# A third of a fused kernel's loads moved to ScalarE's DMA queue, with a new written order of all stages

## The chip, the cores and the metric

The kernel runs on one core of a Trainium2 chip. A core has TensorE (PE in the profile; its weight loads are PEld), VectorE (DVE), ScalarE (ACT), GpSimd (POOL) and SyncE (SP), each with its own instruction queue, and 16 DMA engines that all queues share. Times are device microseconds (us) of one execution, lower is better.

## The reference

Two operations follow each other. The first is a linear attention with a decaying state, for 4 sequences of 768 steps, 8 heads of 48 channels:

```python
for t in range(S):
    cur = einsum('bhd,bhe->bhde', u[None] * kt, vt)
    y[:, :, t] = einsum('bhd,bhde->bhe', rt, state + cur)
    state = w[None, :, :, None] * state + einsum('bhd,bhe->bhde', kt, vt)
```

Its output, with the 8 heads side by side as `x` of 4 x 768 x 384, goes through a gated layer. `conv` is a causal convolution with 5 taps over the steps, each channel by itself:

```python
gate = sigmoid(conv(x, conv_w))
out  = (gate * (x @ w_val)) @ w_out
```

Inputs and output are float32. `r`, `k` and `v` are 4.7 MB each, `w_val` and `w_out` 0.6 MB each, the output 4.7 MB.

## The kernel before, in words

**Tiling.** The 768 steps of each sequence are cut into 3 units of 256 steps, 12 units in all (`n` = 0 to 11), and each unit into two chunks of 128 steps. The state passes from chunk to chunk within a sequence; a new sequence starts at n = 0, 3, 6 and 9.

**One unit.** The loads bring `r` (one transfer of 384 KB), and `k` and `v` (two transfers of 192 KB each, one for each chunk: `k:4.1` is the second half of unit 4). In memory a row of 48 channels is 192 bytes, so a `k` or `v` transfer is 1,024 pieces of 192 bytes; `r` takes two steps in one piece, 1,024 pieces of 384 bytes. Then: `RS` and `KS` multiply `r` and `k` with powers of the decay (L260, L289, on POOL; with a star in the order on DVE). `RT` and `KT` transpose them on PE (L274, L312), `RE` and `KE` copy the result out of PSUM on ACT (L282, L322). `PR`, `S` and `SE` make the factor of the bonus term `u` (L331, L343, L355), `DV` multiplies `v` with it (L358, POOL, with a star DVE). `CV` casts `v` (L298, ACT). `A` makes the scores of a chunk (L372, PE), `M` masks them (L385, DVE, four for each unit). `KV` forms the chunk's part of the state (L399, PE), `ZE` and `ID` decay and add (L416, L411, DVE). `YD` starts the output of both chunks from `DV` (L427, PE), `Y` completes a chunk (L441, PE), `YE` copies it out (L470, ACT). Of the gated layer `C` is the convolution (L485, 40 small matmuls), `SG` the sigmoid (L498, ACT), `V` the value product (L505 and L514), `HT` gate times value (L527, DVE), `O` the output product (L537), `OE` its copy (L549, ACT), and `st` the store of a unit (L553, SP). The last unit does the gated layer in smaller parts (`CL`, `GL`, `VL`, `HL`, `OL`, `XL`, `stl`).

**Beginning.** `w` and `cw` load the decay row and the convolution weights on SP; `wt` and `ut` load small pairs on ACT; `WB`, `LN`, `DRI` and `DKI` make the tables of decay powers (PE, then ACT). Unit 0 runs in halves (`RSP`, `RTP`, `REP`, `KSP`, `KTP`, `KEP`). `Wv` and `Wo` load the two weight matrices, `WV`, `WP` and `WO` cast them. `CWB`, `CWT`, `CWC`, `CWD` prepare the convolution weights (`CWB`, on DVE, is the first to need `cw`). `TL` loads the sigmoid's table on ACT.

**What sets the order.** `ORDER` is a written list of all 555 stages. A loop at the end calls them one by one, and each appends its instructions to the queues of its engines. So the list fixes the order within every queue, and nothing across queues: an instruction starts when its queue has come to it and the semaphores that it waits for have arrived. A load on SP is passed by no other load of SP, but may run long before or after the compute stages that stand beside it in the list. The function `queue` sends a load to ScalarE's queue when its token has a star, else to SyncE's. Such an issue stands in the same queue as ACT's copies and sigmoids.

**Buffers.** There are 7 buffers each for `k` and `v`, 6 for `r`, 11 for output units, and 8 PSUM banks handed out in turn. By the trace's issue records the transfers use 8 completion semaphores in turn, over both queues: an issue also waits until the transfer before it on the same semaphore has landed. For example, the issue of `k:1.1` starts at 4.19 us, and the first half of `r:0`, which had the same semaphore, landed at 4.17 us.

Of the kernel before, what the change touches and what calls it, by code (L numbers as in the profile page):

```python
# [16 lines left out]
def kernel(  # L17
# [14 lines left out]
    B, H, S, D = r.shape  # L32
    C = 128
# [60 lines left out]
    wt = consts.tile([128, NP], F32)  # L94
    nc.vector.memset(wt, 1.0)
    ut = consts.tile([128, NP], F32)
# [28 lines left out]
    st = {}  # L125
# [522 lines left out]
    def store_l(n, cl, half, eng):  # L648
# [3 lines left out]
        eng.dma_start(out=out[b, t0 : t0 + C, c0 : c0 + n0], in_=st["o_l", n, cl, half])  # L652

    ORDER = """
        w wt:0 r:0.0 WB:0 wt:1 r:0.1 cw r:1* CWB WB:1 LN:0 k:0.0 DRI:0 k:0.1 LN:1 ut:1 k:1.1 DKI:0
        k:1.0 DRI:1 RSP:0.0 ut:0 RSP:0.1 CWT RS:1 RTP:0.1 DKI:1 WCT r:2 REP:0.1 k:2.1 k:2.0
        RTP:0.0 v:0.0 v:0.1 v:1.1 v:1.0 r:3 REP:0.0 KSP:0.0 KSP:0.1 WCM Wv k:3.1 v:2.0 UW k:3.0
        v:2.1 Wo k:4.0 RS:2 k:4.1 r:4 KTP:0.0 v:3.0 v:3.1 r:5 KEP:0.0 RT:1 KS:1* KTP:0.1 KEP:0.1
        A:0.0 k:5.1 KS:2 PR:0 M:0.0 k:5.0 r:6 RE:1 KT:1 S:0 A:0.1 PR:1 v:4.0 v:4.1 SE:0 M:0.1 KE:1
        S:1 A:1.1 k:6.0 k:6.1 v:5.0 v:5.1 A:1.0 M:0.3 SE:1 DV:0 r:7 DV:1 RT:2 M:1.3 M:1.2 CWC KT:2  # L660
        M:0.2 CV:0 KV:0.0 RS:3 M:1.1 RE:2 ZE:0.0 WV CV:1 YD:0 M:1.0 KE:2 TL KV:0.1 ZE:0.1 KV:1.0
        ID:1.0 KS:3 YD:1 A:2.0 PR:2 Y:0.1 ZE:1.0 Y:1.0 Y:0.0 YE:0.1 Y:1.1 k:7.1 CWD YE:1.0 A:2.1
        RT:3 KV:1.1 YE:0.0 YE:1.1 C:1 M:2.1 ZE:1.1 V:0.1 RE:3 S:2 SG:1.0 M:2.3 CV:2 M:2.2 C:0
        V:1.0 SE:2 SG:0.0 SG:1.1 SG:0.1 M:2.0 DV:2 HT:1.0 KV:2.0 V:0.0 ID:2.0 WO KT:3 YD:2 V:1.1
        k:7.0 ZE:2.0 v:7.1 HT:1.1 v:6.0 PR:3 KE:3 HT:0.1 WP Y:2.0 Y:2.1 O:1.0 KS:4 O:1.1 HT:0.0
        S:3 YE:2.0 A:3.1 RS:4 OE:1.0 YE:2.1 OE:1.1 SE:3 A:3.0 M:3.1 CV:3 v:6.1 C:2 SG:2.0 RT:4
        O:0.1 SG:2.1 DV:3 M:3.2 RS:5 v:7.0 KV:3.0 KS:5 RS:6 M:3.0 KT:4 V:2.1 RE:4 O:0.0 M:3.3 KE:4
        YD:3 ZE:3.0 KV:3.1 Y:3.1 Y:3.0 OE:0.1 PR:4 HT:2.1 ZE:3.1 A:4.1 A:4.0 RT:5 YE:3.1 OE:0.0
        M:4.3 S:4 V:2.0 SE:4 YE:3.0 M:4.0 M:4.1 r:8 DV:4 RE:5 k:8.1 KT:5 CV:4 C:3 RT:6 PR:5 M:4.2
        KV:4.0 V:3.1 SG:3.0 ID:4.0 YD:4 ZE:4.0 SG:3.1 k:8.0 S:5 KS:6 Y:4.0 SE:5 Y:4.1 KE:5 A:5.0  # L670
        YE:4.0 HT:3.1 YE:4.1 A:5.1 HT:2.0 v:8.0 M:5.1 M:5.2 RE:6 C:4 KT:6 CV:5 O:2.1 DV:5 V:4.0
        M:5.3 KV:4.1 M:5.0 SG:4.0 SG:4.1 YD:5 PR:6 k:9.0 OE:2.1 KE:6 k:9.1 KV:5.0 RS:7 ZE:4.1
        V:3.0 RT:7 S:6 ID:5.0 SE:6 ZE:5.0 KS:7 RE:7 O:2.0 Y:5.0 Y:5.1 HT:3.0 A:6.0 A:6.1 OE:2.0
        DV:6 HT:4.0 KT:7 M:6.0 V:4.1 YE:5.0 M:6.3 RS:8 O:3.0 HT:4.1 O:3.1 YE:5.1 KE:7 CV:6 C:5
        PR:7 A:7.1 OE:3.0 M:6.2 A:7.0 M:6.1 V:5.0 SG:5.0 OE:3.1 M:7.3 S:7 M:7.0 SG:5.1 SE:7 KS:8
        KV:6.0 V:5.1 ZE:6.0 HT:5.1 YD:6 O:4.1 KV:6.1 r:9 HT:5.0 RT:8 M:7.2 v:8.1 Y:6.1 k:10.1 CV:7
        Y:6.0 DV:7 r:10* ZE:6.1 RE:8 KS:9 KV:7.0 O:5.1 YE:6.0 KT:8 M:7.1 v:9.1 O:4.0 OE:5.1 O:5.0
        YD:7 OE:4.1 ID:7.0 PR:8 YE:6.1 RS:9 OE:4.0 KE:8 S:8 k:10.0 ZE:7.0 r:11 KV:7.1 OE:5.0 SE:8
        Y:7.1 Y:7.0 v:9.0 v:11.1 YE:7.1 CV:8 A:8.0 A:8.1 C:6 DV:8 M:8.0 v:10.0 V:6.1 M:8.2 SG:6.1
        v:10.1 ZE:7.1 KT:9 YE:7.0 k:11.1 M:8.3 HT:6.1 V:6.0 RT:9 SG:6.0 k:11.0 YD:8 HT:6.0 M:8.1  # L680
        KV:8.0 ID:8.0 O:6.0 RE:9 KE:9 C:7 ZE:8.0 RS:10 PR:9 Y:8.0 RS:11 Y:8.1 OE:6.0 A:9.0 A:9.1
        SG:7.1 KS:10 SG:7.0 RT:10 YE:8.1 M:9.1 v:11.0 M:9.3 YE:8.0 S:9 SE:9 M:9.2 DV:9 CV:9 M:9.0
        V:7.1 C:8 RE:10 KV:9.0 O:6.1 HT:7.1 V:7.0 KT:10 RT:11 HT:7.0 V:8.0 ZE:9.0 st:5 OE:6.1
        V:8.1 KV:9.1 SG:8.1 SG:8.0 CV:10 PR:10 O:7.1 RE:11 O:7.0 ZE:9.1 KV:10.0 HT:8.1 YD:9 S:10
        Y:9.0 KS:11 KE:10 OE:7.1 Y:9.1 YE:9.0 ID:10.0 SE:10 DV:10 HT:8.0 st:2 ZE:10.0 YE:9.1
        A:10.1 M:10.3 A:10.0 CV:11 C:9 M:10.1 KV:10.1 M:10.2 OE:7.0 KT:11 SG:9.1 V:9.0 PR:11 O:8.1
        KE:11 SG:9.0 OE:8.1 O:8.0 M:10.0 ZE:10.1 KV:11.0 V:9.1 YD:10 OE:8.0 S:11 Y:10.1 HT:9.0
        YE:10.1 SE:11 ID:11.0 st:1 ZE:11.0 Y:10.0 HT:9.1 st:4 st:3 A:11.1 DV:11 A:11.0 M:11.1
        YE:10.0 C:10 M:11.2 M:11.0 O:9.0 V:10.1 st:7 YD:11 SG:10.1 st:8 SG:10.0 HT:10.1 V:10.0
        Y:11.0 HT:10.0 O:9.1 st:0 M:11.3 YE:11.0 O:10.1 OE:10.1 Y:11.1 OE:9.1 VL:11.0 YE:11.1  # L690
        OE:9.0 CL:11.0 GL:11.0 CL:11.1 HL:11.0 O:10.0 GL:11.1 VL:11.1 HL:11.1 st:6 OE:10.0 OL:11.0
        st:9 OLb:11.1 OLa:11.1 XL:11.0 st:10 stl:11.0 XLb:11.1 XLa:11.1 stl:11.1 stl:11.2
    """

    wct = consts.tile([128, NP], F32)
# [136 lines left out]
```

## Time and profile before

| | |
|---|---|
| median of 5 runs | 104.85 us (104.12 to 105.15) |
| the profiled execution | 104.12 us |
| its span, first to last instruction | 102.3 us, so 1.8 us lie around it |
| ACT, DVE and POOL busy | 73.1, 72.6 and 65.8 us |
| loads and stores | 15.35 MB read from HBM, 4.72 MB written |
| big loads (r, k, v, the two weights) | 63: 61 issued by SP, 2 by ACT (`r:1`, `r:10`) |
| last load issued, landed | 76.19 us, 80.78 us (`v:11.0`) |
| last matmul ends | 98.4 us |

All times within the execution are counted from the start of the span. "Busy" of PE is modelled from pipelined matmuls. Of the 40 slices of the page each is 2.56 us long. The DMA share is the time that packets took, over 16 engines; it passes 1 where packets overlap.

### The profile page before, as it was taken

Reading aid. Unit: us, or ns where it says so; the run is one execution under the profiler, and the core shown is the slowest. Engines: PE = TensorE matmul, PEld = TensorE weight load, DVE = VectorE, ACT = ScalarE, POOL = GpSimd, SP = SyncE. Lnnn points to the kernel's source line nnn. Section 1 sums busy time; section 2 is a strip of 40 time slices with the busy share of each in tenths; the row PEclk is TensorE's granted clock in tenths of the full one; section 3 lists DMA queues with packets and bytes.
Section 4 is the critical chain, followed back from the end, with each engine's and each line's share of the span. In section 5 each row is a group of like instructions: output and inputs, shape, how many; then the busy total and the mean of one; then the engine's idle time right before and its main releaser. Section 6 shows DMA issues by size and latency. Waiting matters only on the chain.

```text
span 102.3 us, 4626 instructions
## 1 busy us (share of the span) xinstructions
PE 85.1 (83%) x2017; PEld 70.2 (69%) x2017; DVE 72.6 (71%) x145; ACT 73.1 (71%) x126; POOL 65.8 (64%) x67
## 2 busy tenths in 40 slices
PE   1425969369969889999989999996999999999940
PEld 1224759249869678799858796785889788986720
DVE  4058799767537794899959998497697697984320
ACT  5476744595886699798968949968898986636730
POOL 7969298299878687979756269599597660500000
PEclk9999999975999999999999999999999999999996
DMA  0999999998979989999979899899899994372471
GB/s 5 265 211 177 228 186 189 289 222 152 298 135 253 207 174 225 200 165 211 171 139 241 167 211 242 173 193 205 172 180 227 382 345 175 116 270 87 154 276 34
DMA packets 67504, 20.36 MB, mean 199 GB/s; under 512 B 63510, under 2 KB 67484, under 8 KB 67484
## 3 DMA queue, kind: packets, MB, share of 16 engines
q1 hardware_dynamic: 64428, 19.18, 88.2%
q10 hardware_dynamic: 3056, 0.89, 4.0%
q8 instruction: 15, 0.25, 1.1%
q14 instruction: 5, 0.04, 0.1%
HBM read 15.35 MB, written 4.72 MB: 196 GB/s over the span
## 4 chain that ended last, share of the span: by engine, by line
PE 49%; SPq 15%; DMA 14%; ACT 8%; issue 4%; POOL 3%; DVE 2%; POOLq 0%
SPq L69 13%; DMA v_st<-in_v_dram 11%; PE bank L441 9%; PE bank L485 9%; PE bank L537 6%; PE bank L505 5%; PE bank L274 3%; PE bank L427 3%; DMA r_st<-in_r_dram 3%; POOL dv L358 3%; ACT xT L470 2%; PE bank L514 2%; PE bank L372 2%; PE bank L312 2%; PE bank L399 2%
## 5 line engine op out<-in xcount | busy, mean ns | idle before, releaser
L385 DVE TENSOR_TENSOR at<-bank,mask 128x512 bf16<-128x512 f32 x48 | 30.9, 681 | 3.4 <-PE bank L372 3.3
L260 POOL TENSOR_TENSOR rs<-r_st,dr 128x768 bf16<-128x768 f32 x11 | 20.2, 1834 | 6.2 <-DMA r_st<-in_r_dram 6.2
L358 POOL TENSOR_TENSOR dv<-v_st,s_sb 128x768 bf16<-128x768 f32 x12 | 17.7, 1478 | 9.6 <-DVE s_sb L355 5.2
L289 POOL TENSOR_TENSOR ks<-k_st,dk 128x768 bf16<-128x768 f32 x10 | 18.2, 1822 | 6.6 <-DMA k_st<-in_k_dram 4.5
L282 ACT COPY rT<-bank 128x1024 bf16<-128x1024 bf16 (+1 forms) x13 | 15.9, 1234 | 3.8 <-PE bank L274 3.8
L322 ACT COPY kT<-bank 128x1024 bf16<-128x1024 bf16 (+1 forms) x13 | 12.5, 959 | 5.4 <-PE bank L537 1.8
L527 DVE TENSOR_TENSOR hT<-bank,gate 128x384 bf16<-128x384 f32 x22 | 11.8, 551 | 3.6 <-PE bank L514 2.3
L470 ACT CAST xT<-bank 128x384 bf16<-128x384 f32 x24 | 11.1, 487 | 4.1 <-PE bank L441 4.1
L537 PE MATMUL bank<-wout,hT 128*128 128x384 bf16 x66 | 13.4, 327 | 0.0
L298 ACT CAST vb<-v_st 128x768 bf16<-128x768 f32 x12 | 10.0, 836 | 4.2 <-DMA v_st<-in_v_dram 4.2
L498 ACT ACTIVATE gate<-bank 128x384 bf16<-128x384 f32 x22 | 10.0, 494 | 2.5 <-PE bank L485 2.3
L485 PE MATMUL bank<-xT,cwd 64*64 64x128 bf16 (+1 forms) x440 | 11.3, 244 | 0.5 <-ACT xT L470 0.4
L505 PE MATMUL bank<-xT,wval 128*128 128x256 bf16 x66 | 10.8, 273 | 1.0 <-issue 0.9
L549 ACT COPY o_sb<-bank 128x384 f32<-128x384 f32 x22 | 10.7, 500 | 1.2 <-PE bank L537 1.2
L485 PEld LDWEIGHTS <-cwd 64*64 64x64 bf16 x440 | 9.8, 106 | 1.9 <-issue 1.0
L372 PE MATMUL bank<-rT,kT 48*128 48x128 bf16 x192 | 9.2, 236 | 1.0 <-ACT kT L322 0.7
L312 PE MATMUL bank<-ident,ks 128*128 128x128 bf16 x96 | 8.8, 242 | 1.3 <-DVE ks L289 1.3
L441 PE MATMUL bank<-at,vb 128*32 128x128 bf16 x384 | 9.9, 235 | 0.0
L331 DVE TENSOR_TENSOR pr<-bank,rT 128x1024 bf16<-128x1024 bf16 (+1 forms) x13 | 8.3, 644 | 1.9 <-ACT kT L322 1.3
L274 PE MATMUL bank<-ident,rs 128*128 128x128 bf16 x96 | 8.6, 242 | 1.2 <-DVE rs L260 1.1
L312 PEld LDWEIGHTS <-ks 128*128 128x128 bf16 x96 | 6.7, 109 | 2.4 <-POOL rs L260 1.3
L399 PE MATMUL bank<-vb,ks 128*128 128x96 bf16 x80 | 6.8, 209 | 1.8 <-ACT vb L298 1.8
(80 smaller groups left out, 138.2 us busy)
## 6 DMA issues: line engine op xcount, KB each, us to landing
k_st<-in_k_dram SPq DMA_DIRECT2D x24, 192.0 KB, 5.2
v_st<-in_v_dram SPq DMA_DIRECT2D x24, 192.0 KB, 4.5
out_dram<-o_sb SPq DMA_DIRECT2D x11, 384.0 KB, 4.6
r_st<-in_r_dram SPq DMA_DIRECT2D x9, 384.0 KB, 5.7
r_st<-in_r_dram ACTq DMA_DIRECT2D x2, 384.0 KB, 5.4
wv_st<-in_moe_w_val_dram SPq DMA_DIRECT2D x1, 576.0 KB, 6.8
wo_st<-in_moe_w_out_dram SPq DMA_DIRECT2D x1, 576.0 KB, 5.1
r_st<-in_r_dram SPq DMA_DIRECT2D x2, 192.0 KB, 3.2
```

The costliest lines, as they stand in the source:

```text
L69: eng.dma_start(out=d[n][:, cl], in_=src[b, :, t0 : t0 + C, :].transpose([1, 0, 2]))
L260: eng.tensor_tensor(out=rs_t[n % 2][:, :, ps[0] : ps[1], :, 0:D].rearrange("p s n a d -> p (n a) s d"), in0=r_st[n][:, hs], in1=dr[:, hs], ...
L282: nc.scalar.copy(out=st["rT", n][:, ps[0] : ps[1], :].rearrange("x n (i s) -> x s n i", s=2), in_=st["r_tr", n, ps[0]],)
L289: eng.tensor_tensor(out=ks_t[n % 3][:, cs, :, :, 0:D].rearrange("p c n a d -> p c (n a) d"), in0=k_st[n][:, cs], in1=dk[:, cs], op=ALU.mult,)
L312: nc.tensor.transpose(tr[:, c, p, :], ks[:, cls[0] + c, p].rearrange("p a x -> p (a x)"), ident,)
L358: eng.tensor_tensor(out=dv_t[n % 2].rearrange("p c (h d) -> p (c h) d", d=D), in0=v_st[n].rearrange("p c h d -> p (c h) d"), in1=st["s", n ...
L385: nc.vector.tensor_tensor(out=st["at", n, cl][:, par], in0=st["at_ps", n, cl][par], in1=mask[:, None, :].to_broadcast([128, NP, 128]), op= ...
L441: nc.tensor.matmul(out=y_ps[32 * q : 32 * q + 32, T, :], lhsT=lt, rhs=rh, start=False, stop=last, skip_group_check=True,)
L470: nc.scalar.copy(out=xT_t[b % 2][:, :, t0 : t0 + C], in_=st["y_ps", n, cl])
L485: nc.tensor.matmul(out=g_ps[i][64 * qo : 64 * qo + 64, o0 : o0 + n0], lhsT=cwd[rows, T, t, :], rhs=xT[rows, T, t0 + c0 + t : t0 + c0 + t + ...
L505: nc.tensor.matmul(out=v_ps[:, 0:W], lhsT=wval[:, kt, i, :], rhs=xT[:, kt, t0 : t0 + W], start=(kt == 0), stop=(kt == NT - 1), skip_group_ ...
L537: nc.tensor.matmul(out=o_ps, lhsT=hT[:, i, c0 : c0 + C], rhs=wout[:, k, :], start=(j == 0), stop=(j == 2),)
```

## The change

Nothing but `ORDER` changes: the same 555 tokens, in another order, and 19 more of them with a star. No function and no tile changes.

**Queues.** ScalarE issues 19 of the 63 big loads in place of 2: `r:1 k:2.1 k:2.0 r:4 k:3.1 v:2.1 k:4.1 v:3.1 k:5.1 r:5 k:6.1 v:6.1 k:7.1 v:7.1 r:10 k:10.1 v:9.0 v:10.1 v:10.0`, in this order. SyncE keeps 44. Besides, `RS:4` and `DV:6` go from POOL to DVE (`KS:1` was there before).

**Order.** Every stage moves. The tokens of SP's loads, which stood far ahead of the compute stages in the list, stand later in it. `cw` and `CWB` come later, `wt:0` too; `r:1` is ACT's first load, ahead of `wt` and `ut`; three stores (`st:3`, `st:4`, `st:1`) stand beside the last loads of `v`. The diff, cut:

```diff
-        w wt:0 r:0.0 WB:0 wt:1 r:0.1 cw r:1* CWB WB:1 LN:0 k:0.0 DRI:0 k:0.1 LN:1 ut:1 k:1.1 DKI:0
-        k:1.0 DRI:1 RSP:0.0 ut:0 RSP:0.1 CWT RS:1 RTP:0.1 DKI:1 WCT r:2 REP:0.1 k:2.1 k:2.0
-        RTP:0.0 v:0.0 v:0.1 v:1.1 v:1.0 r:3 REP:0.0 KSP:0.0 KSP:0.1 WCM Wv k:3.1 v:2.0 UW k:3.0
...
-        YD:7 OE:4.1 ID:7.0 PR:8 YE:6.1 RS:9 OE:4.0 KE:8 S:8 k:10.0 ZE:7.0 r:11 KV:7.1 OE:5.0 SE:8
-        Y:7.1 Y:7.0 v:9.0 v:11.1 YE:7.1 CV:8 A:8.0 A:8.1 C:6 DV:8 M:8.0 v:10.0 V:6.1 M:8.2 SG:6.1
...
+        w r:1* ut:1 r:0.0 ut:0 r:0.1 WB:0 WB:1 wt:1 LN:0 DRI:0 RSP:0.0 LN:1 DRI:1 DKI:0 DKI:1
+        k:0.1 RSP:0.1 RTP:0.1 k:0.0 k:1.1 KSP:0.1 k:1.0 wt:0 r:2 REP:0.1 k:2.1* KTP:0.1 RS:1 cw
+        RTP:0.0 KEP:0.1 REP:0.0 KSP:0.0 k:2.0* RT:1 KTP:0.0 KS:1* A:0.1 v:0.0 KT:1 WCT UW KEP:0.0
+        RE:1 A:0.0 PR:0 S:0 M:0.2 M:0.3 v:0.1 KE:1 v:1.1 CWB WCM A:1.1 PR:1 RS:2 SE:0 M:0.0 M:1.2
+        TL M:1.3 M:0.1 A:1.0 v:1.0 S:1 r:3 KS:2 CWT DV:0 SE:1 CV:0 r:4* KT:2 Wv k:3.0 KV:0.0 M:1.1
...
+        PR:7 Y:6.1 YE:6.0 YE:6.1 A:7.1 A:7.0 KS:9 O:5.1 S:7 M:7.2 r:10* OE:5.1 k:10.0 SE:7 M:7.0
+        C:6 DV:7 M:7.3 M:7.1 RT:9 CV:7 SG:6.1 S:8 k:10.1* SE:8 RE:9 KV:7.0 V:6.1 ID:7.0 ZE:7.0
+        KT:9 YD:7 HT:6.1 k:11.0 SG:6.0 V:6.0 PR:9 KV:7.1 KE:9 Y:7.1 Y:7.0 HT:6.0 r:11 YE:7.1
+        ZE:7.1 RS:10 A:8.0 A:8.1 A:9.0 YE:7.0 C:7 M:8.3 O:5.0 CV:8 v:9.1 v:9.0* k:11.1 M:8.0 M:9.1
+        KS:10 SG:7.0 O:6.0 DV:8 SG:7.1 M:9.0 RT:10 OE:5.0 OE:6.0 KV:8.0 M:8.2 M:8.1 S:9 V:7.0
+        V:7.1 RE:10 ID:8.0 SE:9 ZE:8.0 v:10.1* O:6.1 OE:6.1 KT:10 RS:11 KE:10 v:10.0* YD:8 A:9.1
...
+        DV:10 M:10.3 ZE:9.0 M:10.0 SG:8.1 v:11.1 st:4 V:8.1 v:11.0 KV:9.1 ZE:9.1 O:7.0 PR:11
```

## The prediction

> **What bounds the kernel now.** First I read the page: the busy shares, the granted clock and the DMA row over the 40 slices.
>
> ```profile
> span 102.3 us, 4626 instructions
> ...
> PE 85.1 (83%) x2017; PEld 70.2 (69%) x2017; DVE 72.6 (71%) x145; ACT 73.1 (71%) x126; POOL 65.8 (64%) x67
> ...
> PEclk9999999975999999999999999999999999999996
> DMA  0999999998979989999979899899899994372471
> ```
>
> No engine but PE is above 71%, and the DMA row is near full until about 80 us. So two things run close together: the loads, and PE. The windows cut the execution where PE becomes dense (21.67), where its clock is full for good (25.40) and where its last matmul ends.
>
> ```profile
> 0.00:21.67 21.67, 11.73 (x122) 9.46 (x122) 13.56 (x33) 13.11 (x21) 15.45 (x36) 1.00 1.16 199
> 21.67:25.40 3.73, 3.73 (x114) 3.27 (x114) 3.33 (x5) 2.80 (x5) 3.73 (x3) 0.54 0.92 153
> 25.40:98.50 73.10, 69.67 (x1790) 57.48 (x1782) 55.67 (x108) 56.88 (x101) 46.62 (x30) 1.00 0.90 205
> ```
>
> The first number pair in each row after the length is PE's busy time. From 25.40 on PE idles only 73.10 - 69.67 = 3.4 us. Before 21.67 it idles 9.9 us and does 122 of its 2,017 matmuls. In the second row the clock is 0.54 of full: some 1.7 us of PE's time are lost there. Hence the end of the kernel is the moment at which PE becomes dense, plus a fixed amount of PE work (about 72 us at full clock for what is left at 21.67), plus PE's later idling, plus a tail of 4 us (last matmul 98.4, span 102.3).
>
> What sets that moment is in the chain of work in order of time, and in SP's timeline beside it.
>
> ```profile
> 14.15 5.82 DMA v_st<-in_v_dram
> ...
> 20.14 1.49 POOL dv L358
> ...
> 21.67 0.55 PE bank L427 x6
> ```
>
> ```profile
> 2.58 4.51 SPq L69 DMA_DIRECT2D k_st<-in_k_dram  x4
> 7.13 1.02 SPq L76 DMA_DIRECT2D r_st<-in_r_dram  x1
> 8.20 2.22 SPq L69 DMA_DIRECT2D k_st<-in_k_dram  x2
> 10.46 4.69 SPq L69 DMA_DIRECT2D v_st<-in_v_dram  x4
> ```
>
> The last of the four `v` halves of units 0 and 1 is issued at 14.15, lands at 19.98, POOL multiplies it until 21.62, and `YD:1` opens PE's dense stretch. The loads stand one behind another on SP at 1.0 to 1.2 us each; the first two took 0.42 and 0.58, so later issues are held back by transfers before them.
>
> **The change, part by part.** The sum is made against the profiled execution (104.12, span 102.3, 1.82 around it) and carried to the median of the runs shown, which is 0.73 higher.
>
> *The beginning.* In SP's queue the two `k:2` issues (2.22 us) leave the place ahead of `v`, and `cw` (0.40) comes in: `v:1.0` is issued up to 1.8 us earlier. If SP's issuing were the limit, PE would be dense 1.8 us sooner. If the 16 engines are, nothing is won: `r:0, r:1, k:0, k:1, r:2, k:2, v:0, v:1` have to pass in both orders. The DMA share is 1.35 at 10 to 13 us and 1.42 at 13 to 16, so the engines are the nearer row. A loss is possible too: `r:4` is now issued by ACT after `CV:0` (16.7 us in before) and takes half of the engines while `v:1.0` finishes, at worst 1.8 us. Range -1.8 to +1.8. I take -0.6, for the queue that is not blocked and for this wait, which goes away because `CWB` leaves the head of DVE's queue:
>
> ```profile
> DVE cw5b L223 <- DMA cw<-in_moe_conv_w_dram: 2.9, 1, 2.9
> ```
>
> It let `RSP:0.0` start only at 5.79, though its table (`DRI:0`) was ready at 4.99 and `r` at 4.17; next late is `DRI:1` and the first `k` half, so 0.8 us at most move on.
>
> *19 loads on ACT.* The row for one in mid-run is `r:10`:
>
> ```profile
> 58.44 0.47 ACT L549 COPY o_sb<-bank 128x384 f32<-128x384 f32 x1
> 58.49 0.40 ACTq L76 DMA_DIRECT2D r_st<-in_r_dram  x1
> 58.80 0.51 ACT L498 ACTIVATE gate<-bank 128x384 bf16<-128x384 f32 x1
> ```
>
> The issue takes 0.40 and lies beside the copy; the sigmoid starts 0.36 after the copy, as copies do without an issue between. So 17 more issues of 0.40 to 0.47 are 7 to 8 us of ACT's sequencer, hidden behind the running copy. I take 0. Without that cover, with about half of them on PE's path, it is +3.4 us.
>
> *The transfers.* The stream is as long as before: 49,152 pieces of 192 bytes and 12,288 of 384. Around the landing of `r:10`, when both queues had work, the rates are in the first of these rows; the others are its neighbours with SP alone.
>
> ```profile
> 60.30:63.30 3.00, 2.96 (x73) 2.11 (x71) 3.00 (x7) 1.64 (x3) 2.03 (x3) 1.00 1.20 246
> 57.30:60.30 3.00, 2.90 (x81) 2.65 (x74) 3.00 (x8) 2.48 (x6) 1.81 (x1) 1.00 0.86 172
> 63.30:66.30 3.00, 3.00 (x90) 2.34 (x88) 1.46 (x4) 3.00 (x8) 1.92 (x2) 1.00 1.01 193
> ```
>
> 246 GB/s against 172 and 193 looks like a gain of a third, but the pieces of `r` are twice as long, which lifts the rate by itself. The share of 1.20 says at most that engines idle less while one queue is blocked. The Trainium skill speaks against this part (DMA: Bandwidth & Descriptors, "Issuing engines are not separate DMA queues"): queues of different engines share the same 16 DMA engines, so issuing from several saves only issue time; by that rule alone the transfers' term would be 0. From the rows: after 21.67 the share is 0.90, so a tenth of the engines' time is empty, and a second queue could fill some of it. What it is worth to PE is bounded by PE's waits for loads. There is one plain case, `YD:8` waiting for `DV:8`:
>
> ```profile
> 70.70 0.51 PE L427 MATMUL bank<-ident,dv 128*128 128x128 bf16 x6 [0.81 <-POOL dv L358]
> ```
>
> With 0.40 at `YD:1` that makes 1.2; all of PE's idling after 25.40 would be 3.4. I take -0.6. The other end is a rival below.
>
> *Moved vector work.* `RS:4` takes 1.83 on POOL; `KS:1`, the same shape on DVE, 0.96. `DV:6` on DVE has no row: between 0.96 and POOL's 1.48. So DVE gets 1.9 to 2.4 us more and POOL 3.3 less. DVE is busy 9.1 of 10 us at 40 to 50, but a queue with 30 us idle in all finds room for it: 0, at worst +1.5. The three stores ahead of `v:11` delay it by about a us each; `CV:11` came 2.1 us after landing in before and `DV:11` 7 us: 0. The clock window at half speed may fall elsewhere: -1.7 to +1.7, taken as 0.
>
> Sum: -0.6 - 0.6 = -1.2. Profiled 104.12 gives 102.9; against the median, 104.85 gives **103.6**.
>
> **Rivals.** (1) *Coupled queues, slower.* In before SP runs free; nothing that compute does can hold it. In the new order a load of ACT is issued only when ACT comes to it, and by the 8 semaphores in turn no SP load that is eight transfers later can be issued before this one has landed; the other way round, ACT, and with it every copy PE waits for, stands still until the transfer eight before has landed. Against it: an SP load lands 4 to 6 us after issue, some five in flight, and eight are allowed. For it: the new order leaves loads little lead. At `S:5`, `C:5` and `S:8` it has issued 38, 48 and 53 big loads; before had issued 39, 47 and 53 when it reached these stages. So it needs the measured rate and no slip. It decides as soon as a transfer takes over 8 x 1.2 = 9.6 us, or the stream falls two to three loads behind: ACT then waits 2 x 1.2 to 3 x 1.2 = 2.4 to 3.6 us, and the time is 107.3 to 108.5. (2) *The engines are the limit everywhere.* Then the beginning gives nothing, the `YD:8` wait reappears elsewhere, and the time is 103.9 to 105.8; that is also what comes out if the new lists merely exchange places with the old. (3) *The beginning gives all*, with the cold clock window gone: -1.8 - 0.8 - 0.6 and some of the 1.7: 101 to 102.
>
> **How the numbers follow.** A change under 1% (1.05 us) cannot be told from none here. Forecast (102.2 to 103.8): 0.32. Rival 3: 0.09. Rival 2: 0.22. Rival 1, including stalls of smaller size from 105.9: 0.37. So faster 0.41, same 0.22, slower 0.37. The range takes in rival 3 down to 101.2 and rival 1 up to 108.2, which leaves some 0.06 below and 0.10 above; the forecast's own is 102.2 to 103.8.
>
> **What would show it.** Right: `YD:1` starts before 21.3; mid-run ACT issues of 0.4 with the next copy not later; PE idles under 3.4 us after its clock is full; the wait of DVE for `cw` is gone. Rival 1 shows as ACT issues that start right at the landing of an earlier transfer while PE waits for `rT`, `kT` or `xT`, or as SP idle before an issue though the DMA share drops below 0.8. Rival 2 shows as a last load at 80 to 81 us and PE dense at 21 to 22. What would make the prediction wrong most: PE idling of more than 6 us after 25, from waits for loads that before had ready.

## The result and the profile after

| | before | after |
|---|---|---|
| median, first comparison | 104.24 us (80 runs, 102.00 to 106.31) | 104.33 us (43 runs, 103.62 to 108.83) |
| median, second comparison, one chip | 103.81 us (35 runs) | 104.31 us (12 runs) |
| ratio after / before | | 1.010 (95%: 1.0078 to 1.0123), then 1.0049 (1.0016 to 1.0081) |
| profiled execution: time, span | 104.12, 102.3 us | 104.69, 102.3 us |
| median span | 101.9 to 102.0 us (four groups of runs) | 102.0 us (both comparisons) |
| time outside the span, median | 1.80 to 2.02 us (the same groups) | 2.34 us (both) |

The two measures differ: by the medians the changed kernel is 0.1 and 0.5 us slower, by the ratios 1.0 and 0.5%. A ratio takes of each kernel only the runs within 1.5% of its fastest, in the first comparison 18 of 80 of the kernel before, which spreads over 4 us, and 35 of 44 of the changed one (its profiled execution counted). So the change costs between nothing and one per cent. Faster, as forecast, it is not. The first thing to see is that the span is the same: what the change wins inside it, it gives back inside it, and some 0.3 to 0.5 us are added outside.

First the page of the changed kernel: the busy shares, the clock and the DMA row in 40 slices.

```profile
span 102.3 us, 4624 instructions
...
PE 84.8 (83%) x2017; PEld 70.0 (68%) x2017; DVE 75.2 (74%) x147; ACT 73.5 (72%) x126; POOL 62.2 (61%) x65
...
PEclk9999999999999999999999999999999999999999
DMA  2999999999999999999999998999999109320723
```

PE has the same 2,017 matmuls and the same busy share. From the second to the 31st slice the DMA row has one 8 and otherwise 9; before had a 7 or an 8 in seven of them. The DMA engines are busier. Then the same three windows as before (length; busy time and count of PE, PEld, DVE, ACT, POOL; clock, DMA share, GB/s).

```profile
0.00:21.67 21.67, 11.40 (x118) 9.50 (x119) 14.08 (x32) 13.96 (x22) 15.07 (x35) 1.00 1.17 198
21.67:25.40 3.73, 3.73 (x121) 3.30 (x120) 3.09 (x5) 0.77 (x2) 2.45 (x2) 1.00 1.35 232
25.40:98.50 73.10, 69.04 (x1778) 56.97 (x1776) 57.72 (x110) 58.38 (x103) 44.63 (x29) 1.00 0.98 202
```

By 21.67 PE has done 118 matmuls, not more than before (122). From 25.40 on it idles 73.10 - 69.04 = 4.1 us, where before idled 3.4. In the second window ACT does 0.77 us of work in 3.73 us (2.80 before): the first sign of what follows. The clock of the first two rows can't be compared with before: its records begin only at 24.35 us in this profile (18.58 in before).

SP's issues at the beginning, in the timeline (start, duration, line, tile, count):

```profile
4.86 2.33 SPq L69 DMA_DIRECT2D k_st<-in_k_dram  x2
7.23 1.00 SPq L76 DMA_DIRECT2D r_st<-in_r_dram  x1
8.28 1.01 SPq L88 DMA_DIRECT2D cw<-in_moe_conv_w_dram  x1
9.33 4.78 SPq L69 DMA_DIRECT2D v_st<-in_v_dram  x4
```

The four `v` halves start at 9.33 in place of 10.46, and the last lands at 18.75 in place of 19.98. That is the gain that the forecast counted. It is not beyond the spread of executions: two kernels of the experiments have the old list as far as `YD:1` (`RS:4` and `DV:6` of before on DVE; old start, new rest), and in their profiles the last half lands at 19.09 and 18.66, and `YD:1` starts at 20.86 and 20.35 in place of before's 21.67. ACT's queue, in the same stretch, has what it did not count:

```profile
10.22 0.75 ACT L282 COPY rT<-bank 128x512 bf16<-128x512 bf16 x1
10.83 0.39 ACTq L69 DMA_DIRECT2D k_st<-in_k_dram  x1
```

This is `k:2.0`. It stands behind the copy `REP:0.0`, and then waits for the landing of `k:1.0` at 10.81. By now `v:0.0`, `v:0.1` and `v:1.1` have been issued ahead of it (at 9.33, 9.74 and 10.67), and it lands at 16.72 in place of 14.54. POOL shows the price. First `KS:2` in before, then POOL's rows in the changed kernel:

```profile
14.67 1.81 POOL L289 TENSOR_TENSOR ks<-k_st,dk 128x768 bf16<-128x768 f32 x1 [0.25 <-DMA k_st<-in_k_dram]
```

```profile
13.06 1.81 POOL L260 TENSOR_TENSOR rs<-r_st,dr 128x768 bf16<-128x768 f32 x1
16.78 1.80 POOL L289 TENSOR_TENSOR ks<-k_st,dk 128x768 bf16<-128x768 f32 x1 [1.91 <-DMA k_st<-in_k_dram]
18.54 2.91 POOL L358 TENSOR_TENSOR dv<-v_st,s_sb 128x768 bf16<-128x768 f32 x2
```

`KS:2` waits 1.91 us for `k:2.0` and starts at 16.78 (before: 14.67). Two things stand behind it: `DV:0` and `DV:1` in POOL's queue, and on PE `KT:2`, in the new list ahead of `YD:0` and `YD:1`:

```profile
18.64 1.04 PE L312 MATMUL bank<-ident,ks 128*128 128x128 bf16 x8 [2.36 <-POOL ks L289]
```

PE waits 2.36 us here and is dense from then on; `YD:1` comes at 21.95 (with the old beginning: 21.67, 20.86 and 20.35). `v:1.0` landed 1.2 us sooner than in the profile of before, but `DV:1` starts only 0.16 us sooner (19.98 against 20.14), behind `KS:2` and `DV:0`: the chain from `k:2.0` over `KS:2` and `KT:2` took the place of the one from `v:1.0`.

The second place is ACT's timeline after 20 us.

```profile
20.89 1.31 ACT L282 COPY rT<-bank 128x1024 bf16<-128x1024 bf16 x1
24.75 0.37 ACTq L69 DMA_DIRECT2D v_st<-in_v_dram  x1
25.16 1.25 ACT L470 CAST xT<-bank 128x384 bf16<-128x384 f32 x3 [2.96 <-PE bank L441]
26.38 0.45 ACTq L69 DMA_DIRECT2D k_st<-in_k_dram  x1
26.87 0.48 ACT L470 CAST xT<-bank 128x384 bf16<-128x384 f32 x1 [0.46 <-PE bank L399]
27.16 2.82 ACTq L69 DMA_DIRECT2D v_st<-in_v_dram  x1
27.25 1.33 ACT L282 COPY rT<-bank 128x1024 bf16<-128x1024 bf16 x1
30.02 1.64 ACT L498 ACTIVATE gate<-bank 128x384 bf16<-128x384 f32 x4 [1.44 <-PE bank L514]
```

The idle time of 2.96 is put down to PE, but `Y:0.0` had ended before 23.5. What ACT stood at is the issue of `v:2.1`, which starts at 24.75, right after `Wv` has landed (24.73). The next `v` half (`v:3.1`, 27.16) starts 0.02 us after a landing too and then takes 2.82 us itself, in which the sigmoids behind it don't start. PE reaches `V:0.0` at 33.08 (before, in its own order: 30.82).

### The profile page after: what moved, and what is told of

It reads as the page before. It is cut to its first block, busy times and chain, and to the rows that moved or that the text cites. A ratio compares the mean times of both kernels' runs of the same rounds, so it can differ in the third digit from the quotient of the medians.

```text
span 102.3 us, 4624 instructions
## 1 busy us (share of the span) xinstructions
PE 84.8 (83%) x2017; PEld 70.0 (68%) x2017; DVE 75.2 (74%) x147; ACT 73.5 (72%) x126; POOL 62.2 (61%) x65
## 2 busy tenths in 40 slices
DMA packets 67503, 20.35 MB, mean 199 GB/s; under 512 B 63510, under 2 KB 67484, under 8 KB 67484
## 4 chain that ended last, share of the span: by engine, by line
PE 63%; DMA 9%; ACT 7%; issue 6%; DVE 5%; POOL 4%; SPq 1%; ACTq 0%; POOLq 0%; DVEq 0%
PE bank L485 10%; PE bank L537 10%; PE bank L441 7%; PE bank L505 6%; DMA k_st<-in_k_dram 5%; PE bank L274 5%; PE bank L312 4%; PE bank L399 4%; PE bank L427 4%; PE bank L372 3%; DMA wt<-in_w_dram 3%; PE bank L514 3%; DVE hT L527 2%; ACT xT L470 2%; ACT kT L322 2%
## 5 line engine op out<-in xcount | busy, mean ns | idle before, releaser
L260 POOL TENSOR_TENSOR rs<-r_st,dr 128x768 bf16<-128x768 f32 x10 | 19.0, 1902 | 7.9 <-DMA r_st<-in_r_dram 6.7
L358 POOL TENSOR_TENSOR dv<-v_st,s_sb 128x768 bf16<-128x768 f32 x11 | 16.2, 1479 | 10.2 <-DVE s_sb L355 5.4
L470 ACT CAST xT<-bank 128x384 bf16<-128x384 f32 x24 | 10.5, 491 | 5.3 <-PE bank L441 4.6
L298 ACT CAST vb<-v_st 128x768 bf16<-128x768 f32 x12 | 10.1, 840 | 2.7 <-DMA v_st<-in_v_dram 2.7
L274 PEld LDWEIGHTS <-rs 128*128 128x128 bf16 x96 | 6.9, 110 | 5.8 <-POOL rs L260 5.2
```

The lines of the kernel that those rows point to most:

```text
L260: eng.tensor_tensor(out=rs_t[n % 2][:, :, ps[0] : ps[1], :, 0:D].rearrange("p s n a d -> p (n a) s d"), in0=r_st[n][:, hs], in1=dr[:, hs], ...
L274: nc.tensor.transpose(tr[:, s, p, :], rs_t[n % 2][:, s, ps[0] + p].rearrange("p a x -> p (a x)"), ident,)
L358: eng.tensor_tensor(out=dv_t[n % 2].rearrange("p c (h d) -> p (c h) d", d=D), in0=v_st[n].rearrange("p c h d -> p (c h) d"), in1=st["s", n ...
```

## The experiments

In a table first, so that the reader has the numbers side by side. "Ratio" is against the kernel before on the same chip, with its 95% interval; its medians there were 104.26, 104.10, 103.76 and 103.81 us in the four groups. The last two columns are medians over the runs. All but two of these kernels lie within 1.3% of the kernel before, so the medians are read together with the intervals, and causes from the traces.

| kernel | median us | ratio | span us | outside us |
|---|---|---|---|---|
| new order, one queue | 103.84 | 1.0026 (0.9977 to 1.0075) | 101.7 | 2.14 |
| old order, two queues | 119.67 | 1.1536 (1.1387 to 1.1685) | 117.8 | 1.84 |
| `v:2.1`, `v:3.1` back on SP | 104.22 | 1.0121 (1.0034 to 1.0209) | 101.85 | 2.37 |
| `wt:0` early | 104.01 | 1.0049 (0.9999 to 1.0100) | 101.75 | 2.28 |
| three early loads back on SP | 103.68 | 0.9987 (0.9944 to 1.0030) | 101.35 | 2.36 |
| only the three early loads on ACT | 103.90 | 1.0049 (1.0008 to 1.0089) | 101.8 | 2.15 |
| one queue, `RS:4` `DV:6` on POOL | 104.02 | 1.0020 (0.9959 to 1.0081) | 102.2 | 1.80 |
| new start, old rest | 103.12 | 0.9951 (0.9908 to 0.9994) | 101.2 | 1.80 |
| early back, `RS:4` `DV:6` on POOL | 103.57 | 1.0010 (0.9972 to 1.0049) | 101.55 | 2.01 |
| before, `RS:4` `DV:6` on DVE | 105.03 | 0.9982 (0.9894 to 1.0070) | 103.2 | 1.82 |
| old start, new rest | 108.58 | 1.0464 (1.0393 to 1.0535) | 106.75 | 1.80 |
| new start, old rest, `RS:4` on DVE | 104.09 | 0.9986 (0.9940 to 1.0032) | 102.3 | 1.77 |
| `k:2.0` back on SP | 103.83 | 0.9978 (0.9935 to 1.0021) | 101.5 | 2.30 |
| `k:2.1`, `r:4` back on SP | 103.93 | 1.0031 (1.0002 to 1.0060) | 101.65 | 2.29 |
| the changed kernel again | 104.31 | 1.0049 (1.0016 to 1.0081) | 102.0 | 2.34 |
| new start, old rest, again | 103.66 | 0.9993 (0.9958 to 1.0028) | 101.75 | 1.79 |

### Order and queues apart

The theory at first: (A) the second queue moves the loads faster, and PE can't use it. Rivals: (B) the coupling of ACT and loads costs time; (C) the new list is itself the worse one. The new order with the old queues:

```diff
-        k:2.1* k:2.0* r:4* k:3.1* v:2.1* k:4.1* v:3.1* ... v:10.0*
+        k:2.1  k:2.0  r:4  k:3.1  v:2.1  k:4.1  v:3.1  ... v:10.0
```

> The new order, with the big loads back on SP but for r:1 and r:10, as in before. Theory A (the second queue moves the loads faster and the new list needs that; what it wins PE cannot use): the last load lands at 82 to 86 us in place of 81.6, ACT's two long stands at 22 to 30 us (1.7 us for a transfer that had to land first, 1.4 us behind a 2.82 us issue) are gone, and the time is within 1% of the changed kernel, 0 to 2% above before. Theory B (coupled queues cost the time): 1.5% or more faster than the changed kernel, so below before. Theory C (the new list is simply worse, queues do not matter): the same as the changed kernel to 0.5%.

And the old order with the new queues, the same stars on the old list:

> The order of before, with the same 19 big loads starred as in the changed kernel. In that list the loads stand up to 20 us ahead of their real issue, so ACT comes to them early. Theory B: ACT stands at issue after issue until the transfer eight before has landed; 5 to 20% slower than before, with ACT idle before its copies. Theory A, if the 19 issues alone are cheap (0.4 us each, hidden): within 1.5% of before. The rate of the loads with two queues should be above before's in both cases.

In the new order the one queue is the better one, by 0.2 to 0.7% (ratios of 1.0026 against 1.0049 and 1.010, of which the first two have intervals that overlap; 103.84 us against 104.31 and 104.33). By the ranges set beforehand this run alone does not part the theories: B had asked for 1.5%, and the last load lands at 82.85, as A had it. In the old order the second queue costs 15 us. Its ACT timeline, and the PE group that waits for it:

```profile
21.50 3.94 ACTq L76 DMA_DIRECT2D r_st<-in_r_dram  x1
25.48 1.07 ACT L322 COPY kT<-bank 128x512 bf16<-128x512 bf16 x2 [12.82 <-issue]
```

```profile
26.12 0.61 PE L372 MATMUL bank<-rT,kT 48*128 48x128 bf16 x8 [14.13 <-ACT kT L322]
```

In the old list the tokens of the loads stand far ahead of the compute. On ACT they became a row of six issues between two copies, most of them waiting for a landing: the issues at 15.17, 16.21, 19.39 and 21.50 start 0.02 to 0.03 us after landings at 15.15, 16.19, 19.37 and 21.47. ACT made no copy for 12.82 us, PE waited 14.13 us, and the span is 116.3 in place of 102.3. So coupling is real (B), it has no fixed size, and in the new list it is small. (C) finds no support: the new list in one queue is not slower than the old by anything that can be measured (ratio 1.0026, 0.9977 to 1.0075; median 0.4 us lower).

The new order in one queue shows in POOL's timeline what the early chain looks like when `k:2.0` (issued at 10.12, landed at 14.42) stands ahead of the `v` halves in one queue:

```profile
14.67 1.92 POOL L289 TENSOR_TENSOR ks<-k_st,dk 128x768 bf16<-128x768 f32 x1
16.69 1.47 POOL L358 TENSOR_TENSOR dv<-v_st,s_sb 128x768 bf16<-128x768 f32 x1
18.68 1.47 POOL L358 TENSOR_TENSOR dv<-v_st,s_sb 128x768 bf16<-128x768 f32 x1 [0.52 <-DVE at L385]
```

`KS:2` starts at 14.67, `DV:1` at 18.68 (20.14 in before), and `YD:1` at 20.44: 1.5 us sooner than in the changed kernel, 1.2 us sooner than in the profile of before, and within what the old beginning shows in three executions (20.35 to 21.67).

### Two suspects that did little

The two issues at which ACT stood at 24.75 and 27.16 were given back to SP:

```diff
-        v:2.1* ... v:3.1*
+        v:2.1  ... v:3.1
```

> The changed kernel with v:2.1 and v:3.1 alone back on SP: the two issues at which ACT stood long. Theory B: YE:0.0 starts at 23.4 to 24.2 in place of 25.16, the sigmoids of C:1 do not wait for an issue, and the time is 0.5 to 1.5% below the changed kernel. Theory A (PE could not have used it, since its clock is half until 24.35 and the loads of unit 2 come no sooner): within 0.4% of the changed kernel.

`YE:0.0` starts at 23.14 in place of 25.16 and `V:0.0` at 31.12 in place of 33.08, somewhat sooner than expected; yet at `YD:6` 0.29 us are left of it (60.04 against 60.33), less than two executions of the changed kernel differ there, and the time is the same. ACT's standing still here was seen, and cost next to nothing.

In the changed kernel POOL had waited 3.19 us for `wt:0`, which landed at 11.04:

```diff
-        ... k:1.0 wt:0 r:2 ...
+        ... wt:1 wt:0 LN:0 ...
```

> The changed kernel with wt:0 issued by ACT right behind wt:1. POOL then has no wait of 3.2 us before the bonus weight (L705). If that wait sets the start: the r of unit 2 is scaled 0.5 us earlier, the whole is 0.5 to 1% faster than the changed kernel. If the k half of unit 2 on ACT's queue (landed at 16.72) sets it: KS:2 still starts at 16.7 and the time is the same to 0.3%.

`wt:0` lands at 8.90 and the first `uw` runs at 9.71, but `KS:2` still waits for `k:2.0` (16.59), and `YD:1` moves by 0.2 us. The median is 0.3 us lower, the interval leaves open whether that is anything. The run shows one thing more. Here the issue of `k:2.0` has the semaphore of `wt:0`, so it waits for no landing. It starts at 11.37 even so, because a copy ahead of it in ACT's queue, `KEP:0.1`, has waited for PE until 10.94, and it lands at 16.52. A place behind ACT's copies is thus enough to make `k:2.0` late; the landing that it waits for in the changed kernel adds at most 0.6 us (the copy `REP:0.0` ahead of it starts at 10.22).

### The beginning

That left `k:2.1`, `k:2.0` and `r:4`, the three loads that ACT issues before PE is dense.

```diff
-        k:2.1* ... k:2.0* ... r:4*
+        k:2.1  ... k:2.0  ... r:4
```

> The changed kernel with its three earliest loads on ACT (k:2.1, k:2.0, r:4) issued by SP again, at the same places of the list; the other 16 stay on ACT. Theory D (the loss is made at the beginning: in the changed kernel the issue of k:2.0 stands in ACT's queue until k:1.0 has landed, 10.83 us, it lands 2.3 us later than with SP, and KS:2, KT:2, YD:1 follow): YD:1 starts at 20.4 to 20.7 as in the new order with one queue (20.44) instead of 21.95, and the time is 103.3 to 103.9. Theory E (the loss is made in mid-run, where issues and ACT's copies hold each other up): YD:1 is early all the same, but the lead is gone by 45 us (KT:6 later than 50.5) and the time is 104.1 to 104.6.

> The counterpart: the changed kernel with only its three earliest loads (k:2.1, k:2.0, r:4) on ACT beside r:1 and r:10; the other 14 on SP. Theory D: YD:1 starts at 21.6 to 22.0 as in the changed kernel, and the time is 104.1 to 104.6. Theory E: YD:1 is as late, but nothing is lost later, so KT:6 is reached by 50.5 and the time is 103.5 to 103.9.

With the three back on SP, and 16 loads still on ACT, the time is 103.68, and the span 0.65 us shorter than that of the changed kernel. `YD:1` starts at 20.95, not quite at 20.4 to 20.7. With only these three on ACT `YD:1` is as late as in the changed kernel (21.86), but `V:0.0` is reached at 30.24, and the time is 103.90, which is the upper end of theory E's range and below theory D's. So theory D is right on where the loss lies when 16 others are on ACT too; alone, the late beginning is mostly made up.

Which of the three is it? `k:2.0` alone back on SP, and the other two alone:

> The changed kernel with k:2.0 alone on SP again; 18 loads stay on ACT, k:2.1 and r:4 among them. If the loss of the beginning is this one load, which stands behind ACT's copy REP:0.0 and then waits for the landing of k:1.0: KS:2 starts at 14.4 to 15.2 in place of 16.78, YD:1 at 20.4 to 21.0 in place of 21.95, and the time is that of the kernel with all three early loads back, 103.4 to 103.9. If r:4, which takes engine time while v:1.0 finishes, or k:2.1 shares the blame, YD:1 comes at 21.2 to 21.9 and the time is 103.9 to 104.4.

> The counterpart: k:2.1 and r:4 on SP again, k:2.0 stays on ACT. If k:2.0 is the loss, KS:2 starts at 16.3 to 17 as in the changed kernel, YD:1 at 21.5 to 22.0, time 104.1 to 104.6. If the other two carry it, YD:1 is at 20.4 to 21.0 and the time 103.4 to 103.9.

> The changed kernel itself, beside the kernel before and the others on one chip. If it is slower than the kernel before, its median is 0.3 to 1.0 us above that of the kernel before here; if the difference lies in the spread of the kernel before alone, the medians are within 0.2 us. Against the kernel with k:2.0 back: 0.4 to 0.8 us slower by the theory of the beginning, equal without it.

Against the changed kernel on the same chip (104.31) both medians are better: 103.83 with `k:2.0` back, 103.93 with the other two back; the intervals of the ratios still overlap with that of the changed kernel. The first expectation held (`KS:2` at 15.10, `YD:1` at 20.94); its profiled execution is a longer one with a span of 103.4, and is not used beyond the beginning. The second held in its other branch. POOL's timeline with `k:2.1` and `r:4` on SP and `k:2.0` on ACT:

```profile
15.47 1.81 POOL L289 TENSOR_TENSOR ks<-k_st,dk 128x768 bf16<-128x768 f32 x1 [0.83 <-DMA k_st<-in_k_dram]
17.23 2.91 POOL L358 TENSOR_TENSOR dv<-v_st,s_sb 128x768 bf16<-128x768 f32 x2
```

`KS:2` starts at 15.47, not at 16.3 to 17, and `YD:1` at 20.64. Here `k:2.1` keeps SP busy until 9.09, `v:0.0` is issued at 10.11, and ACT issues `k:2.0` at 10.14 without waiting for a landing. It lands at 15.40, which is 1.0 us later than with one queue (14.42), but 1.3 us sooner than in the changed kernel, where `v:0.0` is issued at 9.33 and `k:2.0` at 10.83. So `k:2.0` on ACT is not at fault by itself. It is the pair: with both halves of `k:2` gone from SP, SP runs on to the `v` halves, which pass `k:2.0`. The semaphore adds to it: in the changed kernel `k:2.0` has that of `k:1.0`, which is still on its way, and with `k:2.1` back on SP that of `k:0.0`, which has landed. One of the two halves back in SP's queue mends most of it.

### How far the gain of the beginning carries

In one list the time between two stages can be compared over kernels. The table gives starts from the profiled executions, us.

| stage | after | after, second execution | one queue | early back | only early on ACT |
|---|---|---|---|---|---|
| `YD:1` | 21.95 | 21.85 | 20.44 | 20.95 | 21.86 |
| `V:0.0` | 33.08 | 33.04 | 30.00 | 31.03 | 30.24 |
| `KT:4` | 37.21 | 37.17 | 35.40 | 35.79 | 35.42 |
| `YD:6` | 60.33 | 59.77 | 59.55 | 59.18 | 59.89 |
| `KT:8` | 61.32 | 60.76 | 60.54 | 60.18 | 60.88 |
| `C:10` | 89.93 | 89.24 | 89.07 | 89.81 | 89.35 |

A lead of 3.1 us at `V:0.0` (one queue against after) is 1.8 at `KT:4` and 0.8 at `YD:6`; against the second execution of the same changed kernel only 0.2 are left there. From `KT:8` to `C:10` after takes 28.6 and 28.5 us, one queue and only early on ACT 28.5 each, whatever happened earlier. What is lost is lost between 30 and 60 us: from `V:0.0` to `YD:6` after needs 27.3 and 26.7 us, one queue 29.6, only early on ACT 29.7. PE's idle time is part of it (1.23 and 0.54, then 2.26 and 2.62 us, in different places); the rest is not resolved by the records, in which PE's busy time is modelled. With the three early loads back, the lead is lost at the end instead: 0.99 us before the `KV` at 82.45, behind the cast of a `v` half that ACT issued. That execution is the longest of its kernel (104.58 us); with `RS:4` and `DV:6` on POOL besides, the same wait is 0.43 us.

### The loads' rate

The windows by tens of us, first of before, then of after:

```profile
30.00:40.00 10.00, 9.17 (x197) 7.69 (x197) 6.89 (x13) 8.09 (x14) 7.86 (x7) 1.00 1.01 208
40.00:50.00 10.00, 9.86 (x296) 8.64 (x294) 9.10 (x18) 8.68 (x15) 8.88 (x6) 1.00 1.08 196
50.00:60.00 10.00, 9.40 (x218) 7.72 (x217) 8.62 (x18) 8.50 (x15) 6.00 (x4) 1.00 0.90 178
```

```profile
30.00:40.00 10.00, 9.13 (x216) 7.80 (x218) 7.63 (x16) 9.76 (x16) 7.33 (x5) 1.00 1.35 211
40.00:50.00 10.00, 8.77 (x241) 7.11 (x243) 6.68 (x14) 7.34 (x15) 7.87 (x5) 1.00 1.23 212
50.00:60.00 10.00, 10.00 (x246) 8.24 (x241) 9.44 (x18) 9.76 (x17) 10.00 (x6) 1.00 1.17 201
```

The last two numbers are the DMA share and GB/s. The stream is faster with two queues. Counted from the packets of `r`, `k` and `v` alone, 20 to 70 us moved 8.88 MB in before, 8.70 in the new order with one queue, 9.41 in the changed kernel and 9.41 with the three early loads back: 8% more than the same list in one queue. Over all profiled executions it is 9.24 to 9.41 MB with 16 to 19 loads on ACT (9.24 in the old order, as expected above before's), and 8.35 to 9.18 with two to five. Yet the stream does not end sooner than before: the last load lands at 81.61 us (before: 80.78; new order, one queue: 82.85). It is `v:10.0`, to which ACT comes only at 75.68, though its semaphore was free at 71.19. And the rate is worth nothing that can be measured: the new order takes 103.84 us with one queue, and 103.68 with 16 loads on ACT and the beginning mended (span 0.35 us shorter, time outside it 0.22 us longer).

### The moved vector work

```diff
-        RS:4* ... DV:6*
+        RS:4  ... DV:6
```

> The new order with all loads but r:1 and r:10 on SP, and RS:4 and DV:6 on POOL again (KS:1 stays on DVE). If the move of these two to DVE is worth nothing, as forecast, the time is that of the new order with one queue, 103.6 to 104.1. If DVE lost by taking them, it is 103.0 to 103.5; if POOL could not carry them, RT:4 or YD:6 wait, 0.5 to 1.5 us, and it is 104.4 to 105.4.

> The changed kernel with k:2.1, k:2.0 and r:4 on SP again, and RS:4 and DV:6 on POOL again. Beside the span, the executions so far took 1.80 us with RS:4 and DV:6 on POOL, 2.14 with them on DVE and few loads on ACT, and 2.34 with them on DVE and 16 to 19 loads on ACT. If the two vector operations set this, it is 1.8 to 2.0 here, the span stays at 101.2 to 101.6, and the time is 103.1 to 103.5. If it is the loads on ACT, it is 2.3 and the time 103.6 to 103.9. If POOL can't carry RS:4 (a PE wait of 1.5 us at RT:4, as in the new order with one queue and RS:4 on POOL), the span grows by up to 1.5.

The other way round, on the list before:

> The kernel before with nothing but RS:4 and DV:6 on DVE. If the two operations set the time beside the span, it is 2.1 here in place of 1.8. Within the span the forecast was 0, at worst +1.5: DVE is busy 9.1 of 10 us between 40 and 50, so an M or HT that comes 1 us later would show as a PE wait. Time 104.2 to 104.8 by the forecast; above 105.2 if DVE is delayed.

One queue with the two on POOL is within the measurement of one queue with them on DVE (104.02 and 103.84); in the profile `RT:4` waits 1.47 us for POOL at 29.83, in place of 0.45 for DVE at 28.93. The same edit beside the early loads back gives 103.57 against 103.68. In both pairs the zero is a sum: with the two on DVE the span is shorter by 0.5 and 0.2 us, and the time outside it longer by 0.34 and 0.35. On the list before the median is 1.3 us higher (105.03 against 103.76), between the two ranges expected, and the ratio is 0.998, within 0.989 to 1.007: inconclusive. So the term of 0 stands for the new list and is open for the old one, but the durations behind it don't stand, as the last section shows.

### Beginning and rest exchanged

One queue, the new list up to `YD:1` and the old list for all that is left; and the other way round.

```diff
-        [old list, up to YD:1]  [old list, the rest]
+        [new list, up to YD:1]  [old list, the rest]
```

> The new order up to YD:1 and the old order for all tokens that are left, one queue (only r:1 and r:10 on ACT), RS:4 and DV:6 on POOL. It parts the beginning of the new order from its rest. If the new beginning is the gain (YD:1 at 20.4 in place of 21.67) and the new rest gives it back, this keeps it: last matmul at 97.2 to 97.6 and a time of 102.8 to 103.4. If the rest of the new order is as good as the old, or the lead is lost to something that both share (the loads), the time is 103.6 to 104.2. If the two parts don't fit each other (the old rest asks for loads that the new beginning has not issued), it is 104.5 or more.

> The counterpart of the new beginning with the old rest: the old order up to YD:1, the new order for all tokens that are left, only r:1 and r:10 on ACT, RS:4 and DV:6 on DVE. If beginning and rest add up (new beginning -1.2 at YD:1; new beginning with old rest about 1.0% under the kernel before, new order in one queue 0.4% under it), the new rest costs 0.6% and this is 104.5 to 105.0. If the new order's parts only fit each other, it is 105.5 or more. If the new rest is in truth no worse, 103.9 to 104.3.

> The new order up to YD:1 with the old rest, as before, once more beside the others. If its gain is real: 0.6 to 1.0 us under the median of the kernel before and under the changed kernel; if it was chance, within 0.3 us of the kernel before.

The new beginning with the old rest gave 103.12 at first, 0.5% under before with an interval that just leaves out 1. The second time it gave 103.66 and a ratio of 0.9993: most of that gain was chance. It is 0.65 us under the changed kernel beside it, and no better than before by more than can be measured. So the new beginning by itself, with no early load moved to ACT, was worth half a per cent once and nothing in the repeat.

The old beginning with the new rest does not fit together, and says nothing of the rest by itself: the old beginning has issued loads of later units first, `r:4` is issued at 26.37 and lands at 33.74, and `RT:4` waits for it:

```profile
34.85 1.03 PE L274 MATMUL bank<-ident,rs 128*128 128x128 bf16 x8 [6.49 <-DVE rs L260]
```

That wait of 6.49 us is more than all of the 4.6% (4.8 us).

In the first mixture `RT:4` had waited 1.67 us for `RS:4` on POOL, at 37.19. Taking that away by a star:

```diff
-        RS:4
+        RS:4*
```

> The new order up to YD:1 with the old rest, and RS:4 on DVE in place of POOL, where RT:4 had waited 1.67 us for it at 37.19 (POOL came to it at 35.32 only, though its r had landed at 22.38). If that wait is on the path of the end, up to 1.5 us go: 101.6 to 102.6, less 0.2 to 0.3 that the time beside the span may grow. If the next wait takes its place (the next loads, whose landing sets RT:5 and KT:4), the time stays at 102.9 to 103.4.

The wait is gone (`KT:4` at 37.60 in place of 38.30) and the time is 104.09, not lower. `YD:6` is reached at 59.69, against 59.67 and 59.10 in the two executions without the star. So this wait was no price: others took its place.

## Why the prediction was wrong

The forecast was 103.6 against 104.85, a gain of 1.2 us. The median span did not change, and the time rose, by 0.1 and 0.5 us in the medians and by 1.0 and 0.5% in the ratios. The base of 104.85, from five runs, was itself 0.6 us above the median of 80 runs, so that 103.6 as a number says little; the gain is what failed.

**What bounds the kernel: half right.** The end does not follow one for one from where PE becomes dense. "A fixed amount of PE work" holds from `KT:8` on (28.5 to 28.6 us to `C:10` in the kernels of one list where no wait comes in). Between 20 and 60 us most of a lead is given back: 1.5 us at `YD:1` became 0.8 at `YD:6`, or 0.2 by the second execution. What takes it is not resolved.

**The beginning: the step that failed.** "In SP's queue the two `k:2` issues leave the place ahead of `v`: `v:1.0` is issued up to 1.8 us earlier." The issue did come 1.26 us sooner (12.89 against 14.15). But in the 14 profiled executions with the new beginning `v:1.0` lands at 18.38 to 18.78, though its issue starts anywhere from 12.42 to 14.02; with the old beginning it lands at 18.66, 19.09 and 19.98 in three. So the 19.98 on which the step rests was the latest of three, and an earlier issue moved the landing by nothing that shows. The step had named this case itself ("If the 16 engines are, nothing is won"), called it the nearer one by the DMA share, and took -0.6 all the same, together with the wait for `cw`. And it left out the two loads that it took away. They were moved to ACT, and it was not asked when they land there and what waits for them. `k:2.0` landed 2.2 us later than before, `KS:2` started 2.1 us later, and `KT:2` made PE dense at 18.64; `YD:1` came 0.3 us later than in before's profile instead of 0.6 sooner, and 1.5 us later than in the new order with one queue. The wait for `cw` did go away, as forecast, but `RSP:0.0` starts at 5.63 in place of 5.79, so that it was worth 0.16, not up to 0.8: now `RSP:0.0` waits for `r:0.0`, which lands at 5.53 in place of 4.17, with `r:1` issued ahead of it. The worst case that was named, `r:4` taking the engines from `v:1.0`, did not happen: `v:1.0` was not late.

**Nineteen loads on ACT at 0: right in mid-run, wrong at the start.** The row for it was `r:10`, and `r:10` behaves as forecast in the changed kernel: an issue of 0.38 behind the start of a copy of 1.01.

```profile
62.77 1.01 ACT L322 COPY kT<-bank 128x1024 bf16<-128x1024 bf16 x1 [0.94 <-DVE pr L331]
62.84 0.38 ACTq L76 DMA_DIRECT2D r_st<-in_r_dram  x1
63.68 0.87 ACT L470 CAST xT<-bank 128x384 bf16<-128x384 f32 x2
```

Before 32 us five of the eight big loads that ACT issues after `r:1` (`k:2.0`, `k:3.1`, `v:2.1`, `k:4.1`, `v:3.1`) start 0.02 us after a landing, and the 0.4 are the smaller part of what they cost; after that none of this execution does. The row was taken from a place where nothing held the issue.

**Transfers, -0.6: wrong.** Two queues did fill the engines better. The page "DMA: Bandwidth & Descriptors" of the Trainium skill ("Issuing engines are not separate DMA queues") has no gain from several issuing engines but issue time; the runs show 9.41 MB against 8.70 in the same 50 us. They don't tell whether this gain is itself issue time saved: an issue of SP took up to 4.21 us (`Wo` in the changed kernel). But PE's waits for loads were not worth what the forecast gave for them. The wait of `YD:8` is gone (it starts at 75.40 behind another matmul, without a wait), and others came. The term was 0, as by the page, though for another reason.

**Moved vector work at 0:** held in time for the new list, as far as it can be measured; open for the old one. **Clock:** no effect seen, see below.

**The rivals.** Rival 2's number (103.9 to 105.8) is what came out, and its reason, "the new lists merely exchange places with the old", is close. Its "the beginning gives nothing" fits too: the new beginning on the old rest has ratios of 0.9951 and 0.9993, and the six new lists with at least one half of `k:2` back on SP, which start `YD:1` at 20.4 to 21.0, have 0.9978 to 1.0031. Rival 1 had the mechanism that did the harm in both its parts: a load is issued only when ACT comes to it (11.37, with `wt:0` early), and an issue of ACT starts at a landing (10.83 after 10.81, 24.75 after 24.73). The old order with two queues shows it at full size. Its premise that a transfer waits for the one eight before holds in the list before, but not in the new one, as the last section shows. Its price was put too high for the new list, since a hold before 30 us is mostly made up by 60; and it was looked for in the sense that ACT's copies come late, while the costly case was a load that came late.

**What was not foreseen at all** is the time outside the span. The sum carried the 1.82 us of the profiled execution over unchanged. Measured, the median rose from between 1.80 and 2.02 us to 2.34, and these 0.3 to 0.5 us are as large as the whole difference between the medians of the time.

## What to carry to other kernels

When loads are moved to another queue, follow each of the moved loads to its landing and to the instruction that waits for it, not only the loads that move up in the queue they left. Two queues that share completion semaphores are not independent: here it was what stayed in the other queue that decided which load got ahead of which, and one load put back mended most of it. A wait in the middle of a stretch that two resources bound together need not be a price; see if the lead is still there at the end of the stretch. And profile the kernel before more than once: the landing that the first step of this forecast wanted to move was late in that one execution.

## What the runs showed of the hardware

**VectorE and GpSimd hold each other up.** The forecast took 0.96 us for `RS:4` on DVE and 0.96 to 1.48 for `DV:6`. With the star they took 0.96 and 0.96 in the list before, but 1.21 to 2.37 and 0.95 to 2.54 in the new one. In the new order with one queue, POOL's and DVE's timelines:

```profile
26.24 1.82 POOL L289 TENSOR_TENSOR ks<-k_st,dk 128x768 bf16<-128x768 f32 x1
```

```profile
26.50 2.37 DVE L260 TENSOR_TENSOR rs<-r_st,dr 128x768 bf16<-128x768 f32 x1
```

POOL's product ends at 28.06, and DVE's, begun in its course, ends 0.81 us after that: about its own 0.96, counted from the end of the other. The Trainium skill says so (SBUF — State Buffer, "SBUF: two separate sides"): a DVE operation with two SBUF inputs and a GpSimd operation that reads SBUF share a port pair, and whichever starts second waits for the whole of the first. The row agrees. So the price of such a move from POOL to DVE is not the DVE row taken alone, but up to that plus the rest of POOL's operation. The beginning of the changed kernel has a case too: its second `RSP` on DVE, at 6.55, took 1.84 in place of 0.56, beside an `RS` on POOL from 6.17 to 7.98. It also works in the other direction: with the three early loads back, a POOL cast of 0.50 us (L246) took 1.24 beside an `RS:4` on DVE.

**Time outside the span** depends on the kernel, and in the whole new lists, but for a single outlier, hardly on the execution: 2.24 to 2.41 us in 44 executions of the changed kernel, 2.10 to 2.18 in 12 of the new order with one queue, 1.74 to 1.83 with `RS:4` and `DV:6` on POOL besides. The kernel before is not so steady: its medians are 1.80 to 2.02 us, single executions 1.72 to 3.26. In whole new lists the time follows these two operations and the number of loads on ACT; in the list before the same two operations left it at 1.82, and in the two mixtures of lists (both on DVE, or `RS:4` alone) at 1.80 and 1.77. The theory that the two operations set it has fallen, and the cause is open.

**Completion semaphores are not always eight transfers apart.** By the issue records of the list before, 61 of the 75 issues that use a semaphore again have that of the transfer exactly eight earlier in the list. In the changed kernel it is 17 of 75, and the distance runs from 2 to 13: `k:2.0` has the semaphore of `k:1.0`, five transfers earlier. So "eight are allowed" in the prediction was too wide for the new list.

**The clock.** The forecast counted some 1.7 us lost at half clock in the first windows. Over 44 executions of the changed kernel the mean clock was under 0.98 in 18; their median span is 101.95 us, that of the others 102.15. The records are incomplete besides: they begin at 24.35 us in the profile of the changed kernel, so that nothing is known of its clock before (the expectation above that takes it as half until then has no record for it). Whether a low clock early on costs nothing or is not fully recorded, it can't be priced from the clock row alone.
